# Four edits in one: weight steps moved to VectorE, another first stretch, one load moved, a third pair of switch tiles from distances

## The chip, the cores and the metric

The kernel runs on one core of one Trainium2 chip. The metric is device time in microseconds (us), the median of three runs: 850.3 us (849.32 to 852.1). One more execution was taken with the profiler; it took 854.13 us, and its trace spans 852.2 us. All rows below come from that one. The engines are TensorE (PE; its weight loads are listed as PEld), VectorE (DVE), ScalarE (ACT), GpSimd (POOL) and SyncE (SP, which here only issues DMAs; ACT issues some too).

## The reference

Attention with a learned position bias feeds a gated two-layer network.

```python
scores = q @ k.T / sqrt(64)                       # B=4, H=8, S=576, D=64
x    = log1p(|i-j|) / log1p(max(i,1))             # one number per (i, j)
bias = relu(x * w1 + b1) @ w2                     # 32 hidden units, 8 heads
attn = softmax(scores + bias) @ v
x    = attn.transpose(0,2,1,3).reshape(2304, 512)
out  = (sigmoid(x @ w_gate) * (x @ w_val)) @ w_out   # 512 -> 1536 -> 512
```

## The kernel before, in words

The kernel has three stages, one behind the other, with pieces of the next one begun inside the one before.

**Bias.** ReLU of a line is the line times a switch that is 0 or 1. So the bias of an (i, j) is a sum over 32 hidden units of switch times (w1 w2 x + b1 w2). A switch tile holds, in 128 partitions, 4 rows i times 32 hidden units, and all 576 columns j in bf16. Rows i come in nine chunks of 64, so 16 switch tiles a chunk, stored as 8 pairs. A tile is made in one of two ways. `one(i)` (L303) multiplies a small table of x in bf16 parts by prepared weights on PE, two matmuls of 288 columns into a PSUM tile `y`, and ACT turns `y` into 0 or 1 with a steep sigmoid (L311; a few in the first chunk go to DVE, L309). `apart(n)` (L313) needs no PE or ACT: DVE compares 16-bit distances with a threshold for each row and unit (`dist` > `edge`, L324, tile `far`). Before, pairs 6 and 7 of the 8 come that way (`DPAIRS`), the other 12 tiles of a chunk by `one`.

The loop over chunks (L374 on) then sums: for each of five blocks of columns (order `BORD` = 0, 1, 4, 2, 3) PE multiplies the switch tiles by the coefficients `cfs`, 48 small matmuls a block (24 for block 4), into a PSUM tile `bps`, of which there are two. `leave` (L332) takes a block out: DVE multiplies the slope part by x (`btmp`, L338, L351) and adds the rest (`bias`, L346); for blocks 0 and 4 ACT first copies the rest (`brest`, L341) and POOL adds (L346, L356). Between the matmuls the tiles of the next chunk are made: at the positions in `YPOS` PE does one `y`, at those in `DPOS` DVE does one `far` piece. After every block `conv` does one step of narrowing six weight blocks ahead (tile `cvm`, L175 to L187).

**Attention.** 16 units of 9 steps, PE-heavy; K and Q are split into a high and a low part (`prep_k`, `prep_q`, L474, L475) one unit ahead. `begun()` in the bias loop steps a generator that starts this work, so the place of a `yield` sets where a load is issued.

**Network.** Six token tiles of 384 times 12 slices f of the hidden width. For a tile and slice, `gates` (L855) does 24 matmuls into `pg` and `pu`, `gated` takes sigmoid on ACT (L863), the product on DVE (`g`, L864), and splits it (`gh` ACT L865, `gl` DVE L866), and `outs` (L876) does nine matmuls into `po`, issued behind the next tile's `gates`. `ps_g` and `ps_u` have one PSUM tile each. 36 weight blocks (12 slices, three matrices) must be unpacked from 64-bit floats. Six were done in the bias stage; the other 30 are done while the first two token tiles (A and B in `ORDER`) are computed. `convert()` steps a pipeline of blocks: size on ACT (L175), clamp on DVE or POOL by `CLENG` (L178), low, top and tail on DVE (L181, L184, L187), `upper` on ACT (L822) and `lower` on the engine that `LOENG` gives (L827). The last two write the high and the low part that PE multiplies. `CONV` gives two convert steps to an A tile and one to a B tile. All engines work their own queue in order; nothing is reordered at run time.

Of the kernel before, what the change touches and what calls it, by code (L numbers as in the profile page):

```python
# [90 lines left out]

def const_tables():
# [16 lines left out]
    pick = np.zeros((4, 32, 15), np.float32)  # L109
    for i in range(27):  # L110
        pick[:, i, ROWS[i // 4][1] if i < 24 else i - 24] = 1.0
        pick[:, i, 3:7] = np.eye(4, dtype=np.float32)[i % 4] if i < 24 else 0.0
        pick[:, i, 7:11] = 0.0 if i < 24 else 1.0
    for r in range(4):
        pick[r, :, 11 + r] = 1.0
# [8 lines left out]
def tile_kernel(ctx, tc, q, k, v, w1, b1, w2, w_gate, w_val, w_out, steps, lpos, xtab, lx, pick, out, phases="0AB"):  # L124
# [7 lines left out]
    with ExitStack() as right, ExitStack() as att:  # L132
# [59 lines left out]
def bias(tc, w1, b1, w2, steps, lpos, xtab, lx, pick, biases, biasL, moe, begun):  # L192
# [6 lines left out]
    with ExitStack() as ph:  # L199
# [44 lines left out]
        for z, (o, col) in enumerate(((wl, 3), (wt, 7))):  # L244
            nc.vector.tensor_tensor(
                out=o, in0=wr[:, z].rearrange("p (o m) -> p o m", o=1).to_broadcast([128, 4, HID]),
                in1=pk[:, col:col + 4].rearrange("p (g o) -> p g o", o=1).to_broadcast([128, 4, HID]), op=ALU.mult)
        nc.vector.tensor_tensor(out=wl, in0=wl, in1=wt, op=ALU.add)
        for part in range(3):
            nc.vector.tensor_copy(out=wh, in_=wl)  # L250
            if part == 0:
                nc.vector.tensor_scalar(out=wt, in0=wh, scalar1=pk[:, 0:1], scalar2=None, op0=ALU.mult)
            else:
                nc.vector.scalar_tensor_tensor(out=wt, in0=wh, scalar=pk[:, part:part + 1], in1=wt, op0=ALU.mult, op1=ALU.add)
            if part < 2:
                nc.vector.tensor_tensor(out=wl, in0=wl, in1=wh, op=ALU.subtract)
        for r in range(4):
            nc.vector.tensor_scalar(
                out=wy[:, r], in0=wt.rearrange("p g m -> p (g m)"), scalar1=pk[:, 11 + r:12 + r], scalar2=None, op0=ALU.mult)
        cf = cp.tile([128, 2, H, 4], F32, name="cf")  # L260
        nc.gpsimd.memset(cf, 0.0)
        for g in range(4):
            r = slice(32 * g, 32 * g + 32)
            for ab in range(2):
# [701 lines left out]
```

## Time and profile before

| | |
|---|---|
| median of three runs | 850.3 us (849.32 to 852.1) |
| profiled execution | 854.13 us, span 852.2 us, 1.9 us around it |
| PE busy | 804.8 us, 94% |
| DVE, ACT, POOL busy | 522.1, 428.8, 335.1 us |
| mean granted clock of TensorE | 0.982 |

Busy shares are averages over stages that are bound by different engines, and a modelled end of pipelined matmuls makes a PE look busier than it is. So the stages are read apart.

### The profile page before, as it was taken

What the parts mean: (1) busy time and instruction counts of PE and PEld (TensorE: products, weight loads), DVE (VectorE), ACT (ScalarE), POOL (GpSimd) and SP (SyncE); (2) the same over time, 40 slices, a digit from 0 to 9 for tenths busy, and PEclk for the clock granted to TensorE, in tenths of its full rate; (3) what the DMA queues carried; (4) which work ended last, traced back from release to release, by engine and by line L of the source; (5) the groups of instructions that cost most, each with busy time, mean ns of one, the idle gap of its engine ahead of it and who ended that gap; (6) DMA issues with size and microseconds to landing.
All of it is one profiled execution on the core that took longest, in us unless ns stands there. A gap on an engine that the chain in (4) does not pass through costs nothing.

```text
span 852.2 us, 16999 instructions
## 1 busy us (share of the span) xinstructions
PE 804.8 (94%) x6500; PEld 749.6 (88%) x6500; DVE 522.1 (61%) x1059; ACT 428.8 (50%) x912; POOL 335.1 (39%) x360
## 2 busy tenths in 40 slices
PE   4999989999999999888999979999999999999998
PEld 1788879999999998878899858999999999999997
DVE  5588878999889989986888894311412331141211
ACT  2788859989899897754444433211221221122112
POOL 1233469999899979751456661000000000000000
PEclk7899999999999999999999999999999999999999
DMA  4433144656646586559612202030120103011000
GB/s 140 133 130 101 64 122 109 182 150 168 173 125 182 148 213 184 167 163 331 207 62 83 88 1 82 21 112 1 38 88 24 34 5 111 1 38 38 1 1 37
DMA packets 51999, 86.41 MB, mean 101 GB/s; under 512 B 6480, under 2 KB 28112, under 8 KB 51920
## 3 DMA queue, kind: packets, MB, share of 16 engines
q1 hardware_dynamic: 49568, 82.45, 33.0%
q10 hardware_dynamic: 2352, 2.90, 1.0%
q8 instruction: 51, 0.84, 0.4%
q14 instruction: 28, 0.23, 0.1%
HBM read 60.08 MB, written 15.80 MB: 89 GB/s over the span
## 4 chain that ended last, share of the span: by engine, by line
PE 65%; DVE 16%; ACT 5%; DMA 5%; issue 5%; POOL 3%; SPq 1%; ACTq 0%; DVEq 0%; POOLq 0%
PE po L876 13%; PE pu L855 13%; PE pg L855 13%; PE sc L538 7%; PE acc L618 7%; PE pt L561 6%; DVE wm L184 5%; PE bps L330 2%; PE y L306 2%; ACT ind L311 2%; DVE wm L181 2%; PE pt L581 1%; DMA xin<-xs 1%; DVE btmp L338 1%; DVE g L864 1%
## 5 line engine op out<-in xcount | busy, mean ns | idle before, releaser
L855 PE MATMUL pg<-xhi,w 128*128 128x384 f32 x576 | 160.6, 339 | 7.8 <-ACT g L863 6.7
L864 DVE TENSOR_TENSOR g<-pu,g 128x384 f32<-128x384 f32 x72 | 40.0, 556 | 206.0 <-PE pu L855 201.2
L855 PE MATMUL pu<-xhi,w 128*128 128x384 f32 x576 | 161.1, 340 | 5.1 <-POOL w L827 2.7
L876 PE MATMUL po<-w,gh 128*128 128x512 f32 x432 | 134.6, 393 | 0.0
L545 ACT ACTIVATE en<-en,mn 128x576 f32<-128x576 f32 x144 | 111.6, 775 | 31.8 <-DVE mn L542 30.8
L865 ACT ACTIVATE gh<-g 128x384 fp32r<-128x384 f32 x72 | 37.8, 525 | 158.9 <-DVE g L864 158.9
L855 PEld LDWEIGHTS pg<-xhi,w 128*128 128x128 f32 x576 | 105.4, 189 | 13.3 <-ACT g L863 8.9
L538 PE MATMUL sc<-k,QS 128*128 128x288 f32 x640 | 112.8, 302 | 1.7 <-DVE bias L346 0.6
L855 PEld LDWEIGHTS pu<-xhi,w 128*128 128x128 f32 x576 | 105.7, 189 | 8.6 <-POOL w L827 3.7
L542 DVE CUSTOM_DVE_ANT_0 en<-sc,bias 128x576 f32<-128x576 f32 x128 | 93.8, 751 | 7.2 <-PE sc L538 6.1
L855 PE MATMUL pu<-xlo,w 128*128 128x384 f32 x288 | 97.1, 337 | 0.0
L855 PE MATMUL pg<-xlo,w 128*128 128x384 f32 x288 | 97.0, 337 | 0.0
L538 PEld LDWEIGHTS sc<-k,QS 128*128 128x128 f32 x640 | 92.6, 190 | 3.2 <-DVE mn L542 1.0
L561 PE MATMUL pt<-ident,en 128*128 128x128 f32 x576 | 88.0, 276 | 4.1 <-DVE aL L461 1.9
L876 PEld LDWEIGHTS po<-w,gh 128*128 128x128 f32 x432 | 80.7, 189 | 12.2
L863 ACT ACTIVATE g<-pg 128x384 f32<-128x384 f32 x72 | 35.1, 487 | 108.3 <-PE pg L855 108.3
L618 PE MATMUL acc<-aH,vv 128*128 128x288 f32 x256 | 81.6, 335 | 6.2 <-DVE xe L621 3.5
L876 PE MATMUL po<-w,gl 128*128 128x512 f32 x216 | 84.5, 391 | 0.0
L561 PEld LDWEIGHTS pt<-ident,en 128*128 128x128 f32 x576 | 69.3, 142 | 7.3 <-ACT en L545 3.4
L618 PE MATMUL acc<-aL,vv 128*128 128x288 f32 x256 | 71.9, 298 | 0.0
L311 ACT ACTIVATE ind<-y 128x576 bf16<-128x576 f32 x103 | 64.4, 657 | 13.6 <-PE y L306 11.5
L461 DVE TENSOR_TENSOR aL<-pt,aH 128x512 fp32r<-128x512 f32 (+1 forms) x112 | 66.7, 607 | 7.4 <-ACT aH L460 7.4
(113 smaller groups left out, 1506.1 us busy)
## 6 DMA issues: line engine op xcount, KB each, us to landing
kr<-in_k_dram SPq DMA_DIRECT2D x32, 288.0 KB
QS<-part SPq DMA_DIRECT2D x64, 144.0 KB, 2.6
xs<-xe SPq DMA_DIRECT2D x32, 288.0 KB, 3.5
xin<-xs SPq DMA_DIRECT2D x48, 192.0 KB, 3.3
vr<-in_v_dram SPq DMA_DIRECT2D x16, 320.0 KB, 3.5
qr<-in_q_dram SPq DMA_DIRECT2D x16, 288.0 KB
xrec<-rs SPq DMA_DIRECT2D x48, 96.0 KB, 4.0
ww<-in_moe_w_val_dram SPq DMA_DIRECT2D x9, 512.0 KB, 6.5
```

The source lines that it names most:

```text
L184: nc.vector.scalar_tensor_tensor(out=t, in0=hi, scalar=-0x40000000, in1=t, op0=ALU.bitwise_and, op1=ALU.bitwise_or)
L311: nc.scalar.activation(out=o, in_=y[:, :, 0:HF], func=AF.Sigmoid, scale=float(2.0 ** 64))
L461: return lambda: nc.vector.tensor_tensor(out=lo, in0=ps, in1=hi.bitcast(F32), op=ALU.subtract)
L538: nc.tensor.matmul(out=ps[:, e, 0:HF], lhsT=l, rhs=r[:, HF * e:HF * e + HF], start=(i == 0), stop=(i == len(mms) - 1))
L542: nc.vector.tensor_tensor_reduce(out=half(en), in0=ps[:, :, 0:HF], in1=half(nbias), scale=-0.125, scalar=3.0e38, op0=ALU.add, op1=ALU.min, ...
L545: nc.scalar.activation(out=en, in_=en, func=AF.Exp, bias=mn, scale=-1.0, accum_out=sm)
L561: nc.tensor.transpose(pt[:, J], en[:, 128 * J:128 * J + 128], ident)
L618: nc.tensor.matmul(out=acc[:, 0:HF], lhsT=l, rhs=r, start=(i == 0), stop=(i == len(mms) - 1))
L855: self.nc.tensor.matmul(out=(pg, pu)[z], lhsT=l, rhs=r, start=(kc == 0 and i == 0), stop=(kc == 3 and i == 2))
L864: nc.vector.tensor_tensor(out=g, in0=pu, in1=g, op=ALU.mult)
L865: nc.scalar.activation(out=gh, in_=g, func=AF.Copy)
L876: self.nc.tensor.matmul(out=po, lhsT=l[:, tt], rhs=r, start=(f == 0 and i == 0), stop=(f == self.NF - 1 and i == 2))
```

## The change

Four edits. In the network, `LOENG` and `CLENG` give every `lower` and every clamp to DVE (`lower` of slice 0 was there already), the order of the A and B tiles is another (B7 and B8 move ahead of A10), and the loads and splits of token tile 2 (`XAFTER`, while tile 1 runs) come later. In the bias stage, pairs 5, 6 and 7 come from distances in place of 6 and 7, so each chunk has 10 tiles of `one` and 4 pieces of `apart` (three whole pieces and one that joins the ends). In the first stretch, one host-made tensor `small` replaces fifteen small loads, `pos` and `dist` are loaded by ACT's queue, a dummy Exp loads its table, `edges()` comes ahead of the weights, the coefficient arithmetic has fewer and wider instructions, and the `y` tiles of chunk 0 use two `bps` PSUM tiles beside the two `y` tiles (`SIDE`). `load_q(1)` is issued one `begun()` for spreading Q, ahead of splitting K, in place of behind it.

```diff
-YPOS = [18, 22, 26, 30, 34, 38, 46, 52, 57, 62, 67, 72], [3, 9, 15, 21, 27, 33, 39, 45, 52, 58, 66, 72]
-DPAIRS = range(6, 8)
+YPOS = [18, 23, 28, 33, 38, 46, 53, 59, 65, 71], [3, 10, 17, 24, 31, 38, 46, 53, 62, 70]
+DPAIRS = range(5, 8)
-DPOS = [20, 36, 52], [6, 22, 38]
+DPOS = [20, 32, 44, 56], [6, 18, 30, 42]
+SIDE = (2, 3)
-OWN_DVE = (1, 3, 5, 9, 11)
+OWN_DVE = (5, 9, 11, 13)
-ORDER = "A0 A1 B0 A2 B1 A3 B2 A4 B3 A5 B4 A6 B5 A7 B6 A8 A9 A10 A11 B7 B8 B9 B10 B11"
+ORDER = "A0 A1 B0 A2 B1 A3 B2 A4 B3 A5 B4 A6 B5 A7 B6 A8 B7 A9 B8 A10 A11 B9 B10 B11"
+XAFTER = {5: (("l", 0), ("r", 0)), 6: (("l", 1),), 7: (("r", 1), ("l", 2)), 9: (("p", 0), ("p", 1), ("l", 3), ("r", 2)),
+          10: (("p", 2), ("r", 3)), 11: (("p", 3),)}
-LOENG = lambda nc, f, z: nc.vector if f == 0 else nc.gpsimd
-CLENG = lambda nc, f, z: nc.gpsimd if f > 4 and (f + z) % 2 else nc.vector
+LOENG = lambda nc, f, z: nc.vector
+CLENG = lambda nc, f, z: nc.vector
...
+        sm = cp.tile([128, 2 * HID + 17 + H], F32, name="small")
+        nc.sync.dma_start(out=sm, in_=small)
...
+        nc.scalar.dma_start(out=pos, in_=lpos)
+        nc.scalar.dma_start(out=dist, in_=steps)
+        early = cp.tile([128, 1], F32, name="early")
+        nc.gpsimd.memset(early, 0.0)
+        nc.scalar.activation(out=early, in_=early, func=AF.Exp)
...
-            v.tensor_scalar(out=dist, in0=dist, scalar1=sgn, scalar2=None, op0=ALU.mult)
-            v.tensor_scalar(out=pos, in0=pos, scalar1=1000.0, scalar2=None, op0=ALU.min)
-            v.tensor_scalar(out=pos, in0=pos, scalar1=float(2.0 ** 23 - 0.5), scalar2=None, op0=ALU.add)
-            v.tensor_scalar(out=pos, in0=pos, scalar1=float(0.5 - 2.0 ** 23), scalar2=None, op0=ALU.add)
-            v.tensor_scalar(out=edge, in0=pos, scalar1=sgn, scalar2=off, op0=ALU.mult, op1=ALU.add)
+        nc.vector.tensor_scalar(out=pos, in0=pos, scalar1=1000.0, scalar2=half, op0=ALU.min, op1=ALU.add)
+        nc.vector.tensor_scalar(out=edge, in0=pos, scalar1=-half, scalar2=sgn, op0=ALU.add, op1=ALU.mult)
+        nc.vector.tensor_scalar(out=dist, in0=dist, scalar1=sgn, scalar2=off, op0=ALU.mult, op1=ALU.subtract)
...
+                if c == 0 and n % 4 in SIDE:
+                    y = pp.tile([128, 2, 2, H, 32], F32, name="bps").rearrange("p a b h j -> p a (b h j)")
...
     spread_q(0, o)
+    load_q(1)
     yield
...
     load_k(1)
-    load_q(1)
     yield
```

**ACT's queue from its first instruction** (pos and dist are the position tables, ind a switch tile, y and bps PSUM tiles). Before:

```order
L223 DMA wr<-in_b_dram 128x32
L229 DMA wb<-in_b_dram 32x1 x4
L284 ACT_TABLE_LOAD
L284 ACTIVATE pos<-pos,et 128x576
L311 ACT_TABLE_LOAD
L311 ACTIVATE ind_203<-y 128x576
```

And of the change:

```order
L239 DMA pos<-in_lpos_dram 128x576
L240 DMA dist<-in_steps_dram 128x1152
L243 ACT_TABLE_LOAD
L243 ACTIVATE early<-early 128x1
L268 ACTIVATE pos<-pos,et 128x576
L324 ACT_TABLE_LOAD
L324 ACTIVATE ind_179<-y 128x576
L324 ACTIVATE ind_180<-y 128x576
L324 ACTIVATE ind_181<-bps 128x576
```

The first table load no longer stands behind a wait for `pos`, and the third and fourth switch tile leave from `bps`.

**DVE's queue around the start of a later chunk** (cvm are the weight blocks narrowed ahead; L184 and L187, now L197 and L200, are top and tail). Before:

```order
L346 TENSOR_TENSOR bias_73<-bps,btmp 128x2x2x32
L187 SCALAR_TENSOR_TENSOR cvm<-cvw,cvm 128x512
L324 TENSOR_TENSOR far<-dist,edge 128x2x512
L338 TENSOR_TENSOR btmp<-bps,xt 128x512
L324 TENSOR_TENSOR far<-dist,edge 128x2x512
L338 TENSOR_TENSOR btmp<-bps,xt 128x512
```

And of the change:

```order
L359 TENSOR_TENSOR bias_73<-bps,btmp 128x2x2x32
L200 SCALAR_TENSOR_TENSOR cvm<-cvw,cvm 128x512
L337 TENSOR_TENSOR far<-dist,edge 128x2x512
L351 TENSOR_TENSOR btmp<-bps,xt 128x512
L337 TENSOR_TENSOR far<-dist,edge 128x2x512 x2
L351 TENSOR_TENSOR btmp<-bps,xt 128x512
```

The third `far` piece stands right behind the second, between block 0's and block 1's `btmp`.

**DVE's queue in the network, one tile and the convert step behind it** (wm is the block being narrowed, ww its raw form, w the pair of parts). Before, with `lower` (L827) on POOL:

```order
L864 TENSOR_TENSOR g<-pu,g 128x384
L866 TENSOR_TENSOR gl<-g,gh 128x384
L181 TENSOR_SCALAR wm<-wm 128x512
L184 SCALAR_TENSOR_TENSOR wm<-ww,wm 128x512
L187 SCALAR_TENSOR_TENSOR wm<-ww,wm 128x512
L178 TENSOR_SCALAR wm<-wm 128x512
```

And of the change:

```order
L876 TENSOR_TENSOR g<-pu,g 128x384
L878 TENSOR_TENSOR gl<-g,gh 128x384
L839 TENSOR_TENSOR w_10_8382<-wm,w_10_8382 128x512
L194 TENSOR_SCALAR wm<-wm 128x512
L197 SCALAR_TENSOR_TENSOR wm<-ww,wm 128x512
L200 SCALAR_TENSOR_TENSOR wm<-ww,wm 128x512
L191 TENSOR_SCALAR wm<-wm 128x512
```

One instruction more stands in every convert step, and POOL's queue has none behind the end of attention.

## Rows read from the trace of the kernel before

**Rows 1.** The page's busy time of each engine.

```profile
PE 804.8 (94%) x6500; PEld 749.6 (88%) x6500; DVE 522.1 (61%) x1059; ACT 428.8 (50%) x912; POOL 335.1 (39%) x360
```

**Rows 2.** Busy time by stage: start and end of the stretch, its length, then for each engine the busy us and (x instructions), the granted clock, the DMA share and GB/s. The stretches are: up to the first sum of the bias, the bias loop, attention, its hand-over, the network while weights are converted, the rest of the network.

```profile
0.00:24.40 24.40, 11.26 (x36) 4.82 (x37) 12.94 (x42) 7.25 (x9) 3.78 (x16) 0.68 0.41 122
24.40:115.80 91.40, 85.48 (x2138) 77.15 (x2136) 69.80 (x147) 70.77 (x122) 35.22 (x60) 0.99 0.38 115
115.80:375.40 259.60, 249.12 (x1931) 241.90 (x1932) 233.74 (x556) 224.56 (x537) 222.92 (x241) 0.99 0.58 158
375.40:392.40 17.00, 13.40 (x72) 12.89 (x72) 12.23 (x21) 5.43 (x11) 4.36 (x3) 0.90 0.83 264
392.40:515.00 122.60, 111.95 (x563) 99.64 (x562) 107.75 (x140) 48.54 (x93) 67.56 (x40) 0.99 0.35 114
515.00:852.00 337.00, 333.63 (x1768) 313.25 (x1766) 85.64 (x156) 72.23 (x143) 1.29 (x1) 1.00 0.13 40
```

**Rows 3.** Groups of instructions between 392 and 515 us by line and shape: count, then busy us and mean ns of one, then idle time ahead of them and what ended it. The last two rows are from the views of a line over the whole span: count and the shortest, the median and the longest duration in ns.

```profile
L184 DVE SCALAR_TENSOR_TENSOR wm<-ww,wm 128x512 int32<-128x512 int32 x29 | 43.7, 1506 | 1.0
L187 DVE SCALAR_TENSOR_TENSOR wm<-ww,wm 128x512 int32<-128x512 int32 x30 | 27.6, 919 | 1.0
L866 DVE TENSOR_TENSOR gl<-g,gh 128x384 fp32r<-128x384 f32 x17 | 9.5, 559 | 10.0 <-ACT gh L865 10.0
L864 DVE TENSOR_TENSOR g<-pu,g 128x384 f32<-128x384 f32 x17 | 9.3, 549 | 1.9 <-ACT g L863 1.9
...
L178 POOL TENSOR_SCALAR wm<-wm 128x512 f32<-128x512 f32 x11 | 26.1, 2370 | 0.1
...
L178 DVE TENSOR_SCALAR wm<-wm x19: 414/419/829, 390.4 to 506.3; 128x512 f32<-128x512 f32 x19
...
L827 DVE TENSOR_TENSOR w<-ww,w x3: 630/679/1883, 344.1 to 379.0; 128x512 fp32r<-128x512 f32 x3
```

**Rows 4.** The chain of waits just behind 515 us, where only PE is on it: start, length, what.

```profile
515.13 2.05 PE po L876 x9
...
521.35 2.06 PE po L876 x9
```

**Rows 5.** Instructions in order of time in the network: start, duration, engine, line, operation. One on DVE ahead of POOL's work, then a pair of POOL and DVE, then two on DVE around one on POOL.

```profile
391.28 0.69 DVE L184 SCALAR_TENSOR_TENSOR wm<-ww,wm 128x512 int32<-128x512 int32 x1
...
396.64 1.48 POOL L827 TENSOR_TENSOR w<-wm,w 128x512 fp32r<-128x512 f32 x1 [15.85 <-DVE gl L866]
397.01 1.66 DVE L184 SCALAR_TENSOR_TENSOR wm<-ww,wm 128x512 int32<-128x512 int32 x1
...
446.50 0.70 DVE L184 SCALAR_TENSOR_TENSOR wm<-ww,wm 128x512 int32<-128x512 int32 x1
446.87 1.47 POOL L827 TENSOR_TENSOR w<-wm,w 128x512 fp32r<-128x512 f32 x1 [2.02 <-ACT w L822]
447.23 1.66 DVE L187 SCALAR_TENSOR_TENSOR wm<-ww,wm 128x512 int32<-128x512 int32 x1
```

**Rows 6.** The first stretch in order of time, with the idle time ahead of an instruction and what ended it; the last row is from the list of DMA issues of the first 30 us (count, KB each, median us from issue to landing).

```profile
1.16 0.42 SPq L224 DMA_DIRECT2D pk<-in_pick_dram  x1
...
6.34 0.50 DVE L245 TENSOR_TENSOR btmp<-wr,pk 128x128 f32<-128x128 f32 x2 [6.34 <-DMA pk<-in_pick_dram]
...
9.48 0.87 DVE L258 TENSOR_SCALAR wy<-btmp,pk 128x128 bf16<-128x128 f32 x4
...
10.27 0.15 DVE L275 TENSOR_SCALAR et<-wb 128x1 f32<-128x1 f32 x1
...
12.24 1.28 ACT L284 ACT_TABLE_LOAD   x1 [12.24 <-DMA pos<-in_lpos_dram]
...
13.53 0.77 ACT L284 ACTIVATE pos<-pos,et 128x576 f32<-128x576 f32 x1
...
15.62 0.65 ACT L311 ACTIVATE ind<-y 128x576 bf16<-128x576 f32 x1
...
26.62 0.69 DVE L338 TENSOR_TENSOR btmp<-bps,xt 128x512 f32<-128x512 f32 x1 [2.67 <-PE bps L330]
...
w2r<-in_w_dram SPq DMA_DIRECT2D x4, 1.0 KB, 1.5
```

**Rows 7.** The bias loop in order of time: ACT in chunk 0, then DVE and POOL from the last block of one chunk to the last block of the next.

```profile
27.84 3.57 ACT L311 ACTIVATE ind<-y 128x576 bf16<-128x576 f32 x6
...
66.80 0.69 DVE L338 TENSOR_TENSOR btmp<-bps,xt 128x512 f32<-128x512 f32 x1
...
68.20 0.68 DVE L184 SCALAR_TENSOR_TENSOR cvm<-cvw,cvm 128x512 int32<-128x512 int32 x1
...
70.60 0.69 DVE L324 TENSOR_TENSOR far<-dist,edge 128x1024 bf16<-128x1024 f16 x1
...
70.94 1.62 POOL L346 TENSOR_TENSOR bias<-brest,btmp 128x384 f32<-128x384 f32 x2 [4.90 <-ACT brest L341]
...
71.20 0.69 DVE L338 TENSOR_TENSOR btmp<-bps,xt 128x512 f32<-128x512 f32 x1
...
77.25 0.69 DVE L338 TENSOR_TENSOR btmp<-bps,xt 128x512 f32<-128x512 f32 x1
```

**Rows 8.** Where attention begins: one piece of the chain of waits (start, length, what), and ACT's first split of Q.

```profile
113.16 5.49 DMA qr<-in_q_dram
...
119.10 0.69 ACT L474 ACTIVATE part<-qr 128x576 fp32r<-128x576 f32 x1 [0.46 <-issue]
```

More of the change, by code (lines that the diff above doesn't have):

```diff
@@ L71, in host_layout @@
     data["v"] = np.ascontiguousarray(v.transpose(0, 1, 4, 2, 3, 5))
+    w1, b1, w2 = data.pop("w1").reshape(1, HID), data.pop("b1").reshape(1, HID), data.pop("w2")
+    data = {**{n: data.pop(n) for n in "qkv"}, "small": np.ascontiguousarray(np.concatenate(
+        [np.repeat(w1, 128, 0), np.repeat(b1, 128, 0), picks(), np.tile(w1.T, (4, 1)), np.tile(b1.T, (4, 1)), np.tile(w2, (4, 1))],
+        axis=1)), **data}
     return {n: a.view(np.int64) if a.dtype == np.float64 else a for n, a in data.items()}
@@ L89, with picks @@
 ROWS = ((0, 0), (0, 1), (1, 0), (0, 2), (2, 0), (1, 1))
+def picks():
+    pick = np.zeros((4, 32, 15), np.float32)
+    for i in range(27):
+        pick[:, i, ROWS[i // 4][1] if i < 24 else i - 24] = 1.0
+        pick[:, i, 3:7] = np.eye(4, dtype=np.float32)[i % 4] if i < 24 else 0.0
+        pick[:, i, 7:11] = 0.0 if i < 24 else 1.0
+    for r in range(4):
+        pick[r, :, 11 + r] = 1.0
+    return pick.reshape(128, 15)
 def const_tables():
@@ L152, in tile_kernel @@
         with tc.manual_schedule():
-            bias(tc, w1, b1, w2, steps, lpos, xtab, lx, pick, biases, biasL, moe, lambda: next(attn))
+            bias(tc, small, steps, lpos, xtab, lx, biases, biasL, moe, lambda: next(attn))
         if "A" in phases:
@@ L189, in narrow, with bias @@
     return size, clamp, low, top, tail
-def bias(tc, w1, b1, w2, steps, lpos, xtab, lx, pick, biases, biasL, moe, begun):
+def bias(tc, small, steps, lpos, xtab, lx, biases, biasL, moe, begun):
     nc = tc.nc
@@ L209, in load_lx @@
         def load_lx(c):
-            lt = lp.tile([128, len(OWN) // 4, S], BF16, name="lt")
+            lt = lp.tile([128, -(-len(OWN) // 4), S], BF16, name="lt")
             nc.sync.dma_start(out=lt, in_=lx[c].bitcast(BF16))
@@ L243, in bias @@
             nc.tensor.matmul(out=ps[:, i % 2], lhsT=warm[:, 0:128], rhs=warm, start=True, stop=True)
[L244 to L264, printed above, removed]
-                nc.gpsimd.tensor_scalar(out=cf[r, ab, :, g], in0=w2r[r], scalar1=wb[r, ab:ab + 1], scalar2=8.0, op0=ALU.mult, op1=ALU.mult)
-        conv = moe.narrow_ahead(pool("cvw", 2), pool("cvm", 2))
         def edges():
@@ L284, in edges @@
             nc.scalar.activation(out=pos, in_=pos, func=AF.Exp, scale=ratio)
[L285 to L289 removed]
+            return sgn, off
@@ new lines, in bias @@
+        sgn, off = edges()
+        for z, (o, col) in enumerate(((wl, 3), (wt, 7))):
+            nc.vector.tensor_tensor(
+                out=o, in0=wr[:, z].rearrange("p (o m) -> p o m", o=1).to_broadcast([128, 4, HID]),
+                in1=pk[:, col:col + 4].rearrange("p (g o) -> p g o", o=1).to_broadcast([128, 4, HID]), op=ALU.mult)
+        nc.vector.tensor_tensor(out=wl, in0=wl, in1=wt, op=ALU.add)
+        for part in range(3):
+            nc.vector.tensor_copy(out=wh, in_=wl)
+            if part == 0:
+                nc.vector.tensor_scalar(out=wt, in0=wh, scalar1=pk[:, 0:1], scalar2=None, op0=ALU.mult)
+            else:
+                nc.vector.scalar_tensor_tensor(out=wt, in0=wh, scalar=pk[:, part:part + 1], in1=wt, op0=ALU.mult, op1=ALU.add)
+            if part < 2:
+                nc.vector.tensor_tensor(out=wl, in0=wl, in1=wh, op=ALU.subtract)
@@ new lines, in bias @@
+        nc.vector.tensor_scalar(out=dist, in0=dist, scalar1=sgn, scalar2=off, op0=ALU.mult, op1=ALU.subtract)
+        cf = cp.tile([128, 2, H, 4], F32, name="cf")
+        for ab in range(2):
+            nc.gpsimd.tensor_tensor(
+                out=cf[:, ab], in0=w2r.rearrange("p (h o) -> p h o", o=1).to_broadcast([128, H, 4]),
+                in1=group.rearrange("p (o g) -> p o g", o=1).to_broadcast([128, H, 4]), op=ALU.mult)
+            nc.gpsimd.tensor_scalar(out=cf[:, ab], in0=cf[:, ab], scalar1=wb[:, ab:ab + 1], scalar2=8.0, op0=ALU.mult, op1=ALU.mult)
@@ L291, in switches @@
+        conv = moe.narrow_ahead(pool("cvw", 2), pool("cvm", 2))
         def switches(c, lt):
@@ L357, in leave @@
                         out=biasL[64 * e:64 * e + 64, :, j], in0=rest[r, 0, e::2], in1=tmp[r, 0, e::2], op=ALU.add)
-        edges()
         ind, own, far = switches(0, lt)
@@ L363, in bias @@
             f()
-            if far:
+            if far and i in (2, 4, 6, 7):
                 far.pop(0)()
```

39 lines of the change are left out of this document (13 added, 26 removed).

## The prediction

> **What bounds the kernel now.** I read the page's busy times first, then the same by stage, then the chain of waits, then the instructions in order of time where the stages aren't full. PE is busy 94% of the span [rows 1], but by stage [rows 2] that is three things. In attention and in the last 337 us PE is busy all but a few us: nothing beside its own work shortens them. In the first 24.4 us PE does next to nothing. And from 392.4 to 515 us PE is busy 112.0 of 122.6 us, while DVE is busy 107.8.
>
> That last stretch is where most of the change lies. Seventeen tiles are worked off in it (17 `g`) [rows 3]. Where only PE is on the chain a tile takes 521.35 − 515.13 = 6.22 us [rows 4], so 17 take 105.7 us, and 16.9 us are lost. DVE's time there is 107.8 busy, 10.0 waiting between `g` and `gl` for ACT, 1.9 waiting for the sigmoid [rows 3]: 119.7 of 122.6. So DVE bounds it. The reader is to see why in [rows 5]: DVE's `top` (L184) takes 0.69 us with POOL idle, and 1.66 us when it starts 0.37 us behind POOL's `lower`; it ends just when POOL's 1.48 us and its own 0.6 would follow one another. At 446.87 POOL starts inside `top`, and then `tail` behind it is the long one. It is one instruction behind the other, not sharing.
>
> The Trainium skill (SBUF — State Buffer, section "Who interferes with whom") says that a DVE instruction with two SBUF inputs and a GpSimd instruction that reads SBUF exclude each other, whichever starts first holding the ports to its end. The rows above agree with that; the sum needs only the rows.
>
> **The network, term by term.** All on DVE, in the stretch of rows 2 (29 or 30 blocks). What goes: 29 × (1.506 − 0.69) = 23.7 us from `top` and 30 × (0.919 − 0.69) = 6.9 us from `tail`, if POOL's work is gone from there [rows 3, 5]: 30.6 us. What comes: 29 `lower` at 0.68 us, the median of three that DVE did in the old kernel, 19.7 us, and 11 clamps at 0.42 us, 4.6 us [rows 3]: 24.3 us. Net 6.3 us less, so DVE needs 113.4 us for these 29 blocks and 17 tiles. The new order puts two B tiles (B7, B8) ahead of the last blocks. For 19 tiles DVE needs two more times 0.55 + 0.59 + 0.56 = 1.70 us, 116.8 us; PE needs 19 × 6.22 = 118.2 us. So PE becomes the bound, by little; without the new order it would stay DVE. Before, the same 19 tiles cost 122.6 + 12.4 = 135.0. At most 16.9 us are won. I leave 4 us of loss, by the queue: the first blocks of slice 2 are late for A2 as their `lower` now stands behind B0's `g` and `gl` (about 1 us); the last blocks for A11 stand behind A10's `g`, `gl` and three steps of 2 us together (about 2 us); 1 us where the stretch begins, which nothing touches. Behind a waiting `lower` stand `low`, `top`, `tail`, the clamp and the next `g`, and for `g` waits PE's next `pu`. Gain 13 us. Bounds: 16.9 us, or about 1 us if each of 29 `lower` waits for ACT as `gl` does, 0.59 us, 17 us in all. I stay near the top because a `lower` comes one whole convert step behind the `upper` it reads. The three `lower` of slice 1 in the hand-over go to DVE too (2.0 us), where POOL's own contention leaves by about as much; the loads on the chain there are not moved: nothing. The splits for tile 2 move behind B8; the last stands close to its use, hidden or 0.5 us, inside the 4.
>
> **The first stretch.** Old [rows 6]: `pk` is issued at 1.16 us and used at 6.34; the weights `wy` end about 10.3; but ACT only gets `pos` at 12.24, loads a table, does Exp, loads another, and empties the first `y` at 15.62. Twelve tiles then leave through two PSUM tiles, and block 0 is summed at 26.62. New: `small` is the first issue, at about 0.7 us. Its landing isn't shown; `pk`, the nearest, took 5.2 us, a later small load 1.5 us. I take `pk`: 5.9 us. The nine small instructions of `edges` now stand ahead, 9 × 0.15 = 1.3 us, then 9.48 − 6.34 = 3.1 us to the last part, then one wide `wy` of about 0.7 us (a 128x512 `btmp` takes 0.69): 11.0 us, first `y` at 11.6. ACT has its tables by then (two loads and Exp, 3.3 us, run beside DVE's 5 us). ACT empties eight tiles at about 0.6 us (six took 3.57 [rows 7]), to 16.6. DVE has `edge` and `dist` (1.6), three casts and two subtractions (1.0), three whole `far` and the last piece (2.4) and two tiles (1.5): to 17.5. With the rest of block 0, about 1 us, 18.5 in place of 26.6: 8 us. Bounds: 11 with the 1.5 us landing, 5 if `small` comes 3 us later than `pk` did.
>
> **The bias loop.** In chunk 0 ACT sets the pace (six tiles in one run [rows 7]); two tiles fewer is 1.3 us. From chunk 1 on DVE does. One period is 77.25 − 66.80 = 10.45 us. The third `far` piece stands right behind the second and ahead of block 1's `btmp`, for whose `bias` PE waits with the block after next; a `far` adds 0.60 (70.60 to 71.20). Two `y` and two ACT tiles less give back some of it. Bounds −0.6 and +0.6 a chunk; I take +0.2, 1.4 us for chunks 1 to 7. But POOL's two adds start at 70.94, inside the second `far` [rows 7]. The third `far` reads two SBUF tensors like `tail`, and in [rows 5] `tail` came behind the POOL instruction that had come in before it. The first add takes about two thirds of 1.62 us. So where weight narrowing holds DVE up as in this chunk (four chunks, 3 to 6), the third `far` waits about 1 us: 4 us. Together +5 us; bounds −4 and +11.
>
> By the same section of the Trainium skill the third `far`, issued behind a waiting GpSimd instruction, is blocked; that is the 4 us, and a reading without that rule would have +1.4 us in place of +5.
>
> **q ahead of k.** The chain waits 5.49 us for `qr`, issued at 113.16 behind POOL's K splits; ACT stood idle 0.46 us before it could use it [rows 8]. Earlier, that idle time goes: 0.5 us, up to 1; ACT's next Exp is what is late then. Attention itself stays as it is.
>
> **The sum.** −13 − 8 − 1.3 + 5 − 0.5 = −17.8 us. The profiled execution took 854.13 us, so 836.3 for one like it; the median of runs was 850.3, so 832.5.
>
> **Rivals.**
> 1. The long `top` is not POOL's doing. Then 24.3 us come and nothing goes: for 19 tiles DVE needs 119.7 + 24.3 + 3.4 = 147.4 us against 135.0, +12.4, and with the −4.8 of the other stages 857.9: slower. It decides from a refund under 7.6 of the 30.6 us. Against it: the 0.69 at 391.28 and the change of roles at 446.87 [rows 5]; for it, only that `top` is long nearly always.
> 2. DVE waits for ACT at each `lower`, a third of the bound, and PE waits with it: the gain in the network is 5 in place of 13: 840.5. For it: DVE has 1.4 us spare in 118. Against: the step between `upper` and `lower`.
> 3. The third `far` doesn't wait and the two missing tiles pay for it: loop −3 in place of +5: 824.5. For it: PE loses two pairs of matmuls a chunk. Against: POOL's start at 70.94.
> 4. The first stretch gains little, as `small` shares the DMA engines with the tables issued in the same us: 2 in place of 8: 838.5. For it: 5.2 us for `pk`. Against: it is first in its queue.
>
> **How the numbers follow.** My forecast as a case of its own, 827 to 837: 0.57. Rival 3 (822 to 827): 0.13. Rival 2 (837 to 845): 0.15. Rival 4 (837 to 842): 0.09. Rival 1: 0.06. Two in ten may lie outside: rival 1 and the far ends of 2 and 3. Range 821 to 844. A change of under 0.3% (2.6 us) can't be told from none here: slower has rival 1 nearly whole, 0.05; same 0.03, what is left where rivals 2 and 4 meet; faster 0.92.
>
> **What would show it.** In the profile of the change: `top` and `tail` near 0.69 us each and POOL empty behind attention (step 1); DVE's `lower` near 0.68; PE's lost time over the tiles up to A11 at 4 us; the first block's `btmp` near 18.5 us; the period of a chunk 10.7 to 11.7 us, with `far` pieces well over 0.69 us in the middle chunks; ACT's `part` not waiting. The forecast is wrong if `top` stays over 1.2 us, if `small` lands past 9 us, or if the period passes 12 us.

## The result, and the profile after

The changed kernel takes 826.7 us (median of four runs, 824.72 to 828.45); beside it the kernel before took 849.84 us (849.32 to 852.1). The ratio is 0.972, 95% interval 0.969 to 0.975: 23.1 us faster. The prediction was 832.5 us, its range 821 to 844.

The profiled execution of the change took 826.16 us with a span of 824.4. That of before took 854.13, 4.3 us above its median, so the two traces differ by 28.0 us and the medians by 23.1. Over all comparisons below, single executions of before spread from 844.87 to 856.67 us; differences under 3 us need the intervals.

The busy times of each engine, of the change (compare [rows 1]):

```profile
PE 789.9 (96%) x6464; PEld 742.9 (90%) x6464; DVE 513.1 (62%) x1104; ACT 422.7 (51%) x898; POOL 264.6 (32%) x312
```

POOL has lost 70.5 us, but DVE has not gained them: it is 9.0 us less busy. By stage, with the columns of [rows 2]; the stretches are now up to the first sum, the bias loop, attention, hand-over, conversion of weights, rest:

```profile
0.00:12.40 12.40, 8.43 (x32) 3.58 (x33) 8.58 (x33) 7.21 (x11) 2.55 (x12) 1.00 0.70 241
12.40:109.30 96.90, 82.21 (x2107) 75.38 (x2105) 81.36 (x158) 62.39 (x107) 38.50 (x60) 0.98 0.38 111
109.30:361.00 251.70, 244.20 (x1926) 237.98 (x1926) 229.06 (x553) 224.03 (x536) 222.83 (x239) 1.00 0.59 162
361.00:377.00 16.00, 13.83 (x74) 13.24 (x75) 12.23 (x27) 6.43 (x13) 0.73 (x2) 0.89 0.80 242
377.00:500.00 123.00, 121.61 (x640) 112.96 (x639) 99.80 (x187) 53.52 (x97) 0.00 (x0) 1.00 0.39 124
500.00:824.00 324.00, 319.63 (x1693) 299.73 (x1691) 82.09 (x150) 69.15 (x136) 0.00 (x0) 1.00 0.13 40
```

In the conversion stretch PE is now busy 121.6 of 123.0 us, DVE 99.8, POOL not at all. The loop alone got worse: 96.9 us with PE busy 82.2, against 91.4 with 85.5. To see where the time went, the same points are looked up in both traces (`en` is DVE's step that adds the bias to the scores; the `part` here and in [rows 8] is that of unit 1, as unit 0's stands inside the loop):

| point | before | changed | lead | gained since the point above |
|---|---|---|---|---|
| block 0's `btmp` in chunk 0 | 26.62 | 14.59 | 12.0 | 12.0 |
| last block's `btmp`, chunk 0 | 35.76 | 23.06 | 12.7 | 0.7 |
| last block's `btmp`, chunk 7 | 107.82 | 101.21 | 6.6 | −6.1 |
| ACT's `part` of Q for unit 1 | 119.10 | 111.94 | 7.2 | 0.6 |
| 13th unit of attention (its last `en`, from `biasL`) | 311.36 | 303.92 | 7.4 | 0.3 |
| A0's first `pg` | 375.87 | 362.32 | 13.6 | 6.1 |
| A1's first `pg` | 386.47 | 371.46 | 15.0 | 1.5 |
| end of the span | 852.2 | 824.4 | 27.8 | 12.8 |

**The network.** DVE's groups from 377 to 500 us, by line and shape (count, then busy us and mean ns of one, then idle time ahead and its cause; compare [rows 3]):

```profile
L200 DVE SCALAR_TENSOR_TENSOR wm<-ww,wm 128x512 int32<-128x512 int32 x30 | 20.8, 692 | 1.0
L839 DVE TENSOR_TENSOR w<-wm,w 128x512 fp32r<-128x512 f32 x30 | 20.5, 684 | 0.1
L197 DVE SCALAR_TENSOR_TENSOR wm<-ww,wm 128x512 int32<-128x512 int32 x29 | 20.1, 692 | 1.0
L878 DVE TENSOR_TENSOR gl<-g,gh 128x384 fp32r<-128x384 f32 x20 | 11.2, 558 | 11.8 <-ACT gh L877 11.8
L876 DVE TENSOR_TENSOR g<-pu,g 128x384 f32<-128x384 f32 x20 | 11.1, 553 | 9.1 <-PE pu L867 9.1
```

`top` (L197) and `tail` (L200) are at 0.69 us, `lower` (L839) at 0.68, and DVE waits 9.1 us for PE at `g`; before it was 1.9 us for ACT. PE still waits 1.3 us for weights in this stretch, 0.4 at A2 (whose `g` starts at 393.52) and 0.9 at A11 (`g` at 498.09). In order of time, with the idle time ahead and its cause in brackets:

```profile
388.81 0.62 PE L867 MATMUL pu<-xhi,w 128*128 128x384 f32 x2 [0.38 <-DVE w L839]
...
493.58 0.62 PE L867 MATMUL pg<-xhi,w 128*128 128x384 f32 x2 [0.93 <-DVE w L839]
```

**The first stretch**, in order of time (compare [rows 6]; the number in brackets is idle time ahead and its cause):

```profile
3.30 0.15 DVE L259 TENSOR_SCALAR et<-small 128x1 f32<-128x1 f32 x1 [3.30 <-DMA small<-in_small_dram]
...
7.53 0.69 DVE L286 TENSOR_TENSOR wy<-btmp,small 128x512 bf16<-128x512 f32 x1
...
13.14 0.75 DVE L322 TENSOR_SCALAR ind<-y 128x576 bf16<-128x576 f32 x1
14.59 0.69 DVE L351 TENSOR_TENSOR btmp<-bps,xt 128x512 f32<-128x512 f32 x1 [0.71 <-PE bps L343]
```

`small`, issued at 0.73 us, is used at 3.30 (3.26 to 3.61 in six other profiles with it in this place). From there each step stands about where the prediction had it, 2.6 us sooner.

**The loop**, DVE and POOL in the second half of one chunk, and PE's wait for block 1's `bias` (compare [rows 7]):

```profile
67.56 0.68 DVE L351 TENSOR_TENSOR btmp<-bps,xt 128x512 f32<-128x512 f32 x1
...
71.35 2.09 DVE L337 TENSOR_TENSOR far<-dist,edge 128x1024 bf16<-128x1024 f16 x2
73.37 0.68 DVE L351 TENSOR_TENSOR btmp<-bps,xt 128x512 f32<-128x512 f32 x1
...
71.69 2.06 POOL L359 TENSOR_TENSOR bias<-brest,btmp 128x384 f32<-128x384 f32 x2 [5.74 <-ACT brest L354]
...
74.89 0.26 PE L343 MATMUL bps<-cfs,ind 128*128 128x64 bf16 x3 [1.40 <-DVE bias L359]
```

Where POOL does not come in between, in chunks 1 and 2, two `far` pieces take 1.28 us together; here they take 2.09, and POOL's two adds 2.06 in place of 1.62. Periods of chunks 1 to 7 are 10.10, 10.12, 12.88, 11.40, 11.41, 11.38, 10.86 us; before they were 10.15, 10.44, 10.45, 10.45, 10.44, 10.24, 9.89.

**Where attention begins** ACT's `part` has no idle time ahead of it any more (compare [rows 8]):

```profile
111.94 0.67 ACT L486 ACTIVATE part<-qr 128x576 fp32r<-128x576 f32 x1
```

### The profile page after: what moved, and what is told of

Its sections match the earlier page's. It is cut to its first block, busy times and chain, and to the rows that moved or that the text cites. A ratio compares the mean times of both kernels' runs of the same rounds, so it can differ in the third digit from the quotient of the medians.

```text
span 824.4 us, 16845 instructions
## 1 busy us (share of the span) xinstructions
PE 789.9 (96%) x6464; PEld 742.9 (90%) x6464; DVE 513.1 (62%) x1104; ACT 422.7 (51%) x898; POOL 264.6 (32%) x312
## 4 chain that ended last, share of the span: by engine, by line
PE 76%; DVE 14%; DMA 3%; ACT 3%; issue 2%; POOL 1%; SPq 0%; POOLq 0%; DVEq 0%; ACTq 0%
PE pu L867 17%; PE pg L867 17%; PE po L888 16%; PE sc L550 8%; PE acc L630 7%; PE pt L573 6%; PE bps L343 3%; DVE btmp L351 2%; DVE far L337 2%; DVE bias L359 2%; DVE en L554 1%; PE pt L593 1%; DMA xrec<-rs 1%; PE y L319 1%; DVE aL L473 1%
## 5 line engine op out<-in xcount | busy, mean ns | idle before, releaser
L867 PE MATMUL pu<-xhi,w 128*128 128x384 f32 x576 | 159.0, 336 | 0.4 <-DVE w L839 0.4
L557 ACT ACTIVATE en<-en,mn 128x576 f32<-128x576 f32 x144 | 111.6, 775 | 28.7 <-DVE mn L554 27.6
L878 DVE TENSOR_TENSOR gl<-g,gh 128x384 fp32r<-128x384 f32 x72 | 40.2, 558 | 42.6 <-ACT gh L877 42.6
```

The source lines that it names most:

```text
L557: nc.scalar.activation(out=en, in_=en, func=AF.Exp, bias=mn, scale=-1.0, accum_out=sm)
L867: self.nc.tensor.matmul(out=(pg, pu)[z], lhsT=l, rhs=r, start=(kc == 0 and i == 0), stop=(kc == 3 and i == 2))
L878: nc.vector.tensor_tensor(out=gl, in0=g, in1=gh.bitcast(F32), op=ALU.subtract)
```

## The experiments

In all comparisons "before" ran beside the kernel on the same chip. Shares are turned into us with 850.

### Each part alone: e1 to e4

e1 takes the network's lines of the diff into the kernel before (`ORDER`, `XAFTER`, and these):

```diff
+LOENG = lambda nc, f, z: nc.vector
+CLENG = lambda nc, f, z: nc.vector
```

> The kernel before with the network's part of the change alone (lower and clamps on VectorE, B7 and B8 ahead of A10, later splits of token tile 2). Theory 1, the prediction's: POOL's work made top and tail long, so both fall to about 0.69 us and 12 to 14 us go, all between the first tile and the end of the span; from 849.8 to about 837. Theory 2, the network gains less and the rest of what the profile of the change shows there is a lead brought along: under 8 us go. Theory 3 (rival 1): VectorE only gets more work, and the time rises to 855 or more.

Measured: 839.0 us, ratio 0.985 (0.981 to 0.988), 13 us off (10 to 16). `top` and `tail` are at 0.692 us. Theory 1 holds; the 12.8 us in the trace of the change are the network's own.

e2 is the changed kernel with everything but the first stretch put back:

```diff
-DPAIRS = range(5, 8)
+DPAIRS = range(6, 8)
-LOENG = lambda nc, f, z: nc.vector
+LOENG = lambda nc, f, z: nc.vector if f == 0 else nc.gpsimd
...
```

> The kernel before with the edits to the first stretch alone (small, pos and dist on ACT's queue, early table, edges ahead, fewer coefficient instructions, side PSUM tiles), still with two pairs from distances, so 12 tiles of one in chunk 0. Theory 1: the first stretch is worth the 12 us that the profile of the change shows, less what two more tiles cost in chunk 0 (about 1.2 us): block 0's btmp at about 15.5 us and 10.5 to 11.5 us off the whole, to about 839. Theory 2, the prediction's 8 us: about 842. Theory 3, the whole 12 us of the profile hung on the missing tiles: 5 us or less, about 845.

Measured: 839.55 us, ratio 0.986 (0.983 to 0.989), 11.6 us off (9 to 14). Theory 1; the 8 us of theory 2 lie outside the interval. Block 0's `btmp` is at 15.12 us against 14.59 in the change, 0.5 us for two tiles fewer; as a second profile of the change has it at 15.54 (e9), that is within what differs between executions.

e3 takes the third pair alone into the kernel before:

```diff
+YPOS = [18, 23, 28, 33, 38, 46, 53, 59, 65, 71], [3, 10, 17, 24, 31, 38, 46, 53, 62, 70]
+DPAIRS = range(5, 8)
+DPOS = [20, 32, 44, 56], [6, 18, 30, 42]
```

> The kernel before with the third pair from distances alone (10 tiles of one and 4 pieces a chunk, with its own places). Theory 1: VectorE bounds the loop and the third piece waits behind POOL's adds; chunks 1 to 7 get 5 to 7 us longer, chunk 0 about 1 us shorter: 4 to 6 us slower, about 855. Theory 2 (rival 3): the tiles left out pay for it: 1 to 3 us faster. Theory 3: the longer loop of the profile came of its earlier start (loads of the next chunk not landed), not of the third piece: within 1.5 us of before.

Measured: 850.32 us, ratio 0.999 (0.997 to 1.002). Theory 1 had the loop right but not the whole: chunks 1 to 7 got 4.6 us longer and chunk 0 was 0.7 shorter, and the first block's `btmp` came at 24.55 in place of 26.62, 2.1 us that it did not count. In the old first stretch ACT emptied a tile every 1.37 us or more (15.37, 16.74, 18.60 in e3), as each `y` was late, so a tile fewer paid more there than in the new one. Theory 3's number came true, but its reason falls: the longer loop shows without the earlier start.

e4 moves the load of q alone:

```diff
     spread_q(0, o)
+    load_q(1)
     yield
```

> The kernel before with the load of q for unit 1 ahead of the splits of K, alone. Theory 1: only ACT's idle 0.46 us goes, 0.3 to 0.8 us off the whole, about 849.3. Theory 2: the order of the loads also ends the stalls of 300 to 360 us in attention, which were 4 us longer in the profile of before than in that of the change: 4 us or more off the whole. Theory 3: those stalls are another from execution to execution; then the profile of this kernel, whose attention is that of before, shows them at other places or shorter, with no gain in the median.

Measured: 850.87 us, ratio 0.999 (0.997 to 1.001), so no gain over 3 us and none that can be told. That bears against theory 2, whose 4 us or more lie outside the interval, and cannot tell 0.5 us from nothing. The end of attention is taken up under the hand-over below.

### Engines and order apart: e5 and e6

e5 is e1 with the old `ORDER` and no `XAFTER`; e6 is e1 with the old `LOENG` and `CLENG`. What e6 has and e5 has not, `XAFTER` left out here:

```diff
-ORDER = "... B6 A8 A9 A10 A11 B7 B8 B9 B10 B11"
+ORDER = "... B6 A8 B7 A9 B8 A10 A11 B9 B10 B11"
```

> The kernel before with lower and clamps on VectorE alone; the order of A and B tiles and the splits of token tile 2 as before. Theory 1, the prediction's sum: VectorE needs 113.4 us in place of 119.7 for the 17 tiles and stays the bound there: 6 to 8 us off, about 844. Theory 2, the places: before lost 2 us at A1, 4 at A2, 2 between A2 and A8 and 9 from A8 to A11; shorter steps end what is lost ahead of A8 and leave most of the 9: 3 to 5 us off. Theory 3: the engines are the whole gain of the network: 11 us or more off.

> The kernel before with the new order of A and B tiles and the later splits of token tile 2 alone; lower and clamps where they were. Theory 1, the prediction's sum: VectorE needs 119.7 plus 3.4 us for 19 tiles against 135.0 before: 8 to 11 us off, about 841, though top stays at 1.5 us; then with the engines moved it is 12, so the two overlap. Theory 2: the order alone gives 2 us or less, as VectorE's work is what lacks time and that is unchanged. Theory 3: the order is the whole gain: 12 us.

Measured: e5 843.35 us, ratio 0.991 (0.988 to 0.995), 7 us off (4 to 10); e6 844.34 us, ratio 0.990 (0.987 to 0.993), 9 us off (6 to 11). Theory 1's size in both, though e5's interval also admits the top of theory 2. The two overlap: 7 + 9 against 13 together, which the intervals alone can't tell from no overlap, but from A0's `g` to the end of the span the traces of e5, e6 and e1 gain 6.6, 8.2 and 13.0 us. The group of `top` from 392 to 515 us, first of e5, then of e6 (where it is L186):

```profile
L184 DVE SCALAR_TENSOR_TENSOR wm<-ww,wm 128x512 int32<-128x512 int32 x30 | 20.8, 692 | 1.0
```

```profile
L186 DVE SCALAR_TENSOR_TENSOR wm<-ww,wm 128x512 int32<-128x512 int32 x29 | 44.7, 1542 | 1.0
```

With POOL out of the way the same line takes 0.69 us, with POOL there 1.54: the refund of [rows 3] is POOL's doing. What e5 still loses is where theory 2 looked, though smaller. PE's waits from 380 to 525 us in e5:

```profile
PE pg L855 <- DVE w L827: 6.2, 3, 2.7
```

These 6.2 us are three waits of 0.93, 2.64 and 2.66 us at A9, A10 and A11, for `lower`: four A tiles in a row ask for more converted blocks than DVE makes even at its faster pace. In e6 PE's waits for weights come to 1.7 us in the same stretch; two B tiles between the A tiles cure that even with the slow `top`.

### The third pair: e7, e10 and e8

e7 is the changed kernel with two pairs again (the minus lines of `YPOS`, `DPAIRS` and `DPOS` put back).

> The changed kernel with two pairs from distances in place of three (12 tiles of one, the old places in the loop), all else as changed. Theory 1: the third piece costs 6 us in chunks 1 to 7 and gives 1.2 us back before and in chunk 0: 4 to 5.5 us faster than the changed kernel, about 822. Theory 2, after what the kernel before showed with the third pair alone (no difference that can be told): within 1.5 us of the changed kernel, 826.7.

Measured: 827.82 us, ratio 0.972 (0.968 to 0.975), no faster than the change. Yet attention began 4.2 us earlier (first `en` at 106.15, change 110.37), just what the loop was to give. e9 and e10 ran the change and e7 once more, side by side.

> The changed kernel once more, as it is. Theory 1: the time between unit 13 of attention and the first g of the network (67.6 us in the profile of the change, 69 to 76 in the profiles of the other kernels so far) is another from execution to execution, as loads land later or sooner there, so that this profile shows 70 to 75 us and its own time stands above its median, which is 826 to 829. Theory 2: it is the change's own: again 67 to 68.5 us. On chunk 3: if the fall of the granted clock there depends on the moment, its period is 11.4 us this time; if it is the kernel's own, again about 12.9.

> The changed kernel with two pairs once more, on the same chip as the change itself. Its attention began 4.2 us earlier than the change's, and it was no faster. Theory 1: that was the execution, or the chip: beside the change on one chip it is 3 to 5 us faster. Theory 2: what the loop gives is lost again at the hand-over, where the first raw weight block sets ACT's wm, behind which A0's g waits: again within 1.5 us of the change, and that block takes 8 us or more to land.

Measured: e9 827.11 us, ratio 0.973 (0.970 to 0.977); e10 824.22 us, ratio 0.968 (0.964 to 0.972). Again attention began 4.2 us earlier (105.63 against 109.88), and of that 2.9 us arrived in the medians (4.7 by the ratios, whose intervals overlap) and 0.5 in the profiled spans (821.9 and 822.4). Neither theory has it clean: medians and ratios stand near theory 1, the profiles near theory 2. In e10 the first raw block takes 6.78 us to land, in e9 5.39, and by A2's `g` nothing is left (391.7 against 391.4). So the third pair as the change places it costs between nothing (e7) and 3 to 5 us (e10) in all, and in the profiles what it costs in the loop is mostly taken back at the hand-over. For chunk 3, e9 decides for the moment: its period is 11.41 us there, with the same waits and no fall of the clock.

e8 leaves the third pair in and moves its pieces:

```diff
-DPOS = [20, 32, 44, 56], [6, 18, 30, 42]
+DPOS = [20, 32, 44, 56], [6, 18, 34, 44]
```

> The changed kernel with the third distance piece of a chunk moved from position 30 to 34 and the joined ends from 42 to 44, so that block 1's btmp and bias stand ahead of the third piece on VectorE. Theory 1: the 0.8 us that each of five third pieces waits is for POOL's add, which has ended by then: no piece over 0.75 us, PE's wait for block 1's bias shorter by 1.4 us, no fall of the granted clock in chunk 3, period of chunks 4 to 6 about 10.6 in place of 11.4 us: 4 to 6 us faster than the changed kernel, about 822. Theory 2: VectorE's work bounds these chunks and the wait is filled another way: within 1.5 us of it, period still about 11.4.

Measured: 820.03 us (816.69 to 823.55), ratio 0.963 (0.959 to 0.966), 8 us faster than the change by the ratios and the best of all kernels here. The same part of a chunk as above, DVE and POOL of e8:

```profile
67.56 0.68 DVE L337 TENSOR_TENSOR far<-dist,edge 128x1024 bf16<-128x1024 f16 x1
68.17 0.68 DVE L351 TENSOR_TENSOR btmp<-bps,xt 128x512 f32<-128x512 f32 x1
68.88 0.76 DVE L359 TENSOR_TENSOR bias<-bps,btmp 128x384 f32<-128x384 f32 x2
69.55 0.68 DVE L337 TENSOR_TENSOR far<-dist,edge 128x1024 bf16<-128x1024 f16 x1
...
67.90 1.62 POOL L359 TENSOR_TENSOR bias<-brest,btmp 128x384 f32<-128x384 f32 x2 [4.48 <-ACT brest L354]
```

POOL adds while DVE does `btmp` and `bias`, which read PSUM, and both run at their own speed: no piece over 0.69 us, the adds back at 1.62. What PE waits for block 1's `bias` between 23 and 101 us, first in the change, then in e8:

```profile
PE bps L343 <- DVE bias L359: 6.7, 5, 1.4
```

```profile
PE bps L343 <- DVE bias L359: 0.8, 2, 0.6
```

The periods of chunks 4 to 6 are 10.11, 10.13 and 9.98 us, under the 10.6 expected: not just the wait of 0.8 us went, but also part of PE's 1.4, which had come back to DVE as 1.21 us of waiting ahead of block 2's `btmp`. Chunks 1 to 7 take 70.4 us, against 78.2 in the change and 72.1 before. Theory 1 holds and was short. The 8 us rest on the medians and ratios: the profiled execution of e8 is its slowest (823.55 us), and there only 2.6 us of the lead are left at the end (821.8 against 824.4 us); 3.0 are gone between unit 13 and A0, which takes 61.4 us in place of 58.4.

### The hand-over: e11

At the hand-over the chain of waits of the change runs through weights (start, length, what):

```profile
361.88 3.09 DMA ww<-scratch
...
365.00 5.36 DMA ww<-in_moe_w_gate_dram
...
370.38 0.66 ACT wm L188
371.04 0.38 ACT g L875
```

The first convert step puts `wm` on ACT's queue ahead of A0's `g`, so PE's next `pg` waits for a raw 512 KB block. It took 5.36 us here, 7.86 in e8 and 8.53 in e7. e11 is e8 with that step moved behind A0:

```diff
-                for _ in range(CONV[c] - 1 if c < 2 else 0):
+                for _ in range(CONV[c] - 1 if c < 2 and i else 0):
...
                     self.do(START[1], nc.scalar)
+                    self.convert()
```

> The change with the later third piece (e8, 820.0 us), and in the network the first convert step put behind A0's gated and the splits of token tile B, in place of ahead of gated; so ACT's first wm, which waits for a raw weight block, no longer stands ahead of A0's g. Theory 1: PE's wait of 3.7 us for g at A1's pg goes, and the low granted clock behind it: 3 to 6 us faster than e8, about 816. Theory 2: A2 waits for the same weight blocks instead: PE gets A1 earlier and waits as much longer at A2: within 1.5 us of e8.

Measured: 825.08 us, ratio 0.971 (0.968 to 0.973), slower than e8 by 0.8% of before. A0's `g` does come 5.7 us sooner (363.1 against 368.8; 3.1 of it are there at A0's first `pg`, ahead of the edit), but three `wm` now stand in a row ahead of A1's `g`, each waiting for its block, and PE waits there:

```profile
368.81 0.66 ACT L188 ACTIVATE wm<-ww 128x512 f32<-128x512 f32 x1 [2.40 <-DMA ww<-in_moe_w_gate_dram]
373.12 0.66 ACT L188 ACTIVATE wm<-ww 128x512 f32<-128x512 f32 x1 [3.66 <-DMA ww<-in_moe_w_val_dram]
374.86 0.66 ACT L188 ACTIVATE wm<-ww 128x512 f32<-128x512 f32 x1 [1.08 <-DMA ww<-in_moe_w_out_dram]
...
375.95 0.69 PE L867 MATMUL pg<-xhi,w 128*128 128x384 f32 x1 [6.44 <-ACT g L875]
```

That is the mechanism of theory 2, one tile sooner than it said: at B0, for A1's `g`. In the profiles e11 ends 1.1 us behind e8, as theory 2 has it; by the medians it is 5 us behind and by the ratios 7, more than either theory allows, and where the rest is lost is not shown (the two ran on different chips). So the waiting moves with the edit, and what looks to set the hand-over is the blocks themselves.

Why the lead rises by 6.1 us between unit 13 and A0 stays open. From unit 13's `en` to A0's `pg` the profiles show 64.5 us before and 58.4 in the change; 61.0 to 64.5 in the five kernels of e1 to e6 without q ahead, and with it 58.1 to 58.5 in six and 60.5 and 61.4 in two (e7, e8). So e9 repeats the change's figure (theory 2 of e9), and the early load of q looks like the cause. But e4's profile shows 58.1 as well and is among e4's fastest executions (847.99; the twelve span 847.15 to 852.8), with no such gain in its median. A part is the execution that was profiled: without the early load the stretch is the longer, the further the profiled execution lies above its kernel's median (61.0 us at +0.2 in e2, 62.4 at +0.9 in e1, 63.5 at +1.8 in e3, 64.4 to 64.5 at +3.5 to +5.8 in e5, e6 and before). Near the median that leaves up to 4 us for the load of q (61.0 to 62.4 without it, 58.2 to 58.4 with it, but 60.5 in e7), of which e4's interval admits 3; it is not shown. What differs between executions there was not found.

### Where the small load stands: e12

```diff
-        nc.sync.dma_start(out=sm, in_=small)
...
         lt = load_lx(0)
+        nc.sync.dma_start(out=sm, in_=small)
```

> The changed kernel with small issued behind lt on SP's queue (lt is 432 KB) in place of first. In the change small lands 2.55 us after its issue; the prediction took 5.2 from pk, which had stood behind a load in SP's queue and beside many loads of four bytes a row. Theory 1: what is issued ahead sets it: the first et at 5.5 to 7 us in place of 3.3, and block 0's btmp later by about as much (17 to 18 us), the whole 2 to 4 us slower than the change. Theory 2: a load of this form lands in about 2.5 us wherever it stands: et at about 4 us, the whole within 1 us of the change.

Measured: 831.67 us, ratio 0.976 (0.972 to 0.980), 4.6 us slower than the change beside it (e9) by the medians, 2.5 by the ratios, whose intervals overlap. DVE's first instruction and its first `btmp` of a block, in order of time:

```profile
5.58 0.15 DVE L259 TENSOR_SCALAR et<-small 128x1 f32<-128x1 f32 x1 [5.58 <-DMA small<-in_small_dram]
...
17.14 0.69 DVE L351 TENSOR_TENSOR btmp<-bps,xt 128x512 f32<-128x512 f32 x1 [0.71 <-PE bps L343]
```

`small`, issued at 1.18 us behind `lt`, is used 4.4 us later, in place of 2.55, and block 0's `btmp` comes 2.6 us later than in the profile of the change (1.6 later than in e9's). The landing is theory 1's: a load issued ahead sets it. In e12's profile a fall of the clock (below) adds 1.6 us; the rest of the 4.6 is not split further.

## Why the prediction came out as it did

**The network (−13).** Right in size and cause: 12.8 us in the trace, 13 (10 to 16) alone. Of the refund, e5 and e6 show the cause. PE's loss was put at 4 us: 1 at A2, 2 at A11, 1 at the start. From A0's `g` to the first `g` of token tile 2, 24 tiles take 3.4 us more than 24 × 6.22 in the change (2.1 in e9), and 16.7 before, so the 4 and the 16.9 of the sum hold. The two places named were right and half the size: PE waits 0.4 us at A2, 0.9 at A11, and 0.5 for a split of token tile 2 (at 520.78), as the prediction allowed; the rest is not read apart. A reason that fits the shorter waits is that DVE had more room than the sum gave it: busy and waiting for `gh` it comes to 111.6 us for 20 tiles, where 116.8 had been summed for 19. Instructions back to back on DVE overlap: the `far` and `btmp` rows of e8 start 0.61 us apart and last 0.68. The Trainium skill (SBUF — State Buffer, section "Who interferes with whom") says that a DVE instruction with two SBUF inputs and a GpSimd instruction that reads SBUF lock each other out for a whole instruction. The traces agree: 0.69 against 1.54 us for the same `top`.

**The first stretch (−8).** 12.0 us in the profile of the change, 11.1 in that of e9; here the prediction missed most. The step that failed is the landing of `small`: taken from `pk` as 5.2 us from issue, it was 2.55. That is 2.6 of the 4.0 us missed. `pk` had stood behind a load of 16 KB and beside a dozen small ones; e12 puts `small` behind one of 432 KB and gives 4.4, so place in the queue matters, but what made `pk` take 5.2 is not shown. Of the rest 0.8 us is DVE, by the same overlap: from the start of `wy` to the end of its last tile 6.4 us (7.53 to 13.89), where 7.2 had been summed (10.3 to 17.5). The bound of 11 for an early landing is short by the prediction's own terms: a landing after 1.5 us in place of 5.2 takes 3.7 us off, which makes it 11.7 to 11.8.

**The bias loop (−1.3 and +5).** Chunk 0 gave 0.7. Chunks 1 to 7 cost 6.1: 4.6 without the fall of the clock (e3), and 1.5 from it in this execution. The 4 us for the third `far` behind POOL's add were right in mechanism and size, as 5 chunks (3 to 7) at 0.81 us in place of 4 at 1; the 1.4 us for its own work came to 0.5. The Trainium skill's rule (SBUF — State Buffer, section "Who interferes with whom"), against which the reading of +1.4 us stood, is what the rows show. What the prediction missed is that the place, and not the third piece, carries the price: e8 has the piece and loses nothing. So rival 3's reason, that the missing tiles pay, is true in e8 and not in the change.

**q ahead of k (−0.5).** 0.55 us in the trace (6.6 to 7.2); too small for e4's median to confirm. From chunk 7's last `btmp` to `part` it is 11.28 us before and 10.73 in the change. The early load alone gives that (10.73 in e4, 10.74 in e7), but so does the third pair with the load where it was (10.73 in e3, whose loop ends later), so in the change it can't be put down to the load.

**The sum.** The terms as the trace has them give −12.8 − 12.0 − 0.7 + 6.1 − 0.6 = −20.0; the medians give −23.1. The 3 us left belong to the end of attention and the hand-over, which the prediction took to stay and whose cause is open. There the traces differ by 7.9 us; the other 4.9 fit the two profiled executions, which lie 4.3 above before's median and 0.5 below the change's. Of the 5.8 us between forecast and median, 4.0 are the first stretch and 3 the hand-over, and 0.5 is before's median beside the change (849.84 in place of 850.3); 1.8 go the other way, as the loop did worse than forecast, and that these cancel is luck. Alone, e1 to e4 sum to −3.1% and the change has −2.8%, a difference inside the intervals; in the traces the third pair no longer finds, in the changed first stretch, the 2.1 us that it won in e3.

**The rivals.** 1 falls by e5 against e6. 2 falls: DVE waits 0.1 us at 30 `lower`. 4 falls by e2. Rival 3's time, 824.5, was the nearest of all, for another reason than its own.

## What to carry to other kernels

An instruction that GpSimd holds up can be worth more than GpSimd's help: here 24 us of extra work on DVE cost less than the 31 that it had been blocked for, and a row of the blocked instruction at its short and its long duration tells that beforehand. When such an instruction must be added, look for a stretch in which GpSimd works while DVE reads PSUM: four positions later, the same piece went from costing 5 us to costing nothing. And a lead won early can be lost at the next place where data from memory sets the pace: of the 4.2 us that e10 had ahead of attention, its profile kept 0.5.

## What the hardware showed unexpectedly

The granted clock fell in chunk 3 of the change. Rows of stages as above, around PE's 1.40 us wait:

```profile
47.00:50.60 3.60, 1.39 (x30) 1.12 (x27) 3.57 (x7) 3.32 (x7) 2.07 (x2) 0.97 0.64 202
50.60:54.00 3.40, 3.39 (x50) 3.04 (x51) 1.14 (x3) 1.30 (x2) 1.94 (x4) 0.53 0.08 22
54.00:57.00 3.00, 3.00 (x86) 2.81 (x83) 2.50 (x6) 1.53 (x3) 0.00 (x0) 1.00 0.27 69
```

0.53 of full speed is close to the lower level, 1.2 GHz; PE had been busy 1.39 of the 3.60 us before. The same waits (0.82 and 1.40 us) stand in chunks 4 to 6 at a clock of 1.00, in e9's chunk 3 too; in e12 the clock fell in chunk 5 (period 12.99 us). The Trainium skill (TensorE: Matmul & The Clock Gate, section "Part 1: The HAM clock gate") says that the watch over PE's activity runs on its own and does not start with the kernel; that agrees with a fall that comes at another chunk, or at none, from one execution to the next, at 1.5 us each.
